# Segment 0 by query tiles, its first FFN matmul in halves, group priorities in the instruction list, and PSUM pairs as tiles of their own

## The chip, the cores and the metric

The kernel runs on 1 core of one Trainium2 chip. The metric is device time of that core in microseconds (us). A time quoted for a kernel is the median of its runs. Engines: PE is TensorE, PEld its weight loads, DVE VectorE, ACT ScalarE, POOL GpSimd, SP SyncE.

## The reference, cut to what matters

```python
# x: 2048 tokens of 576; 32 heads of 18; 4 segments of 512 tokens
h  = x + A(layernorm(x))                 # memory attention, below
h2 = h + gelu(layernorm(h) @ w1 + b1) @ w2 + b2        # 576 -> 4608 -> 576

# A, for each segment s in order:
p     = softmax(q_s @ k_s.T * scale + causal mask)
a_dot = p @ v_s
a_mem = phi(q_s) @ M / (phi(q_s) @ z + 1e-6)           # M = z = 0 in segment 0
o     = g * a_mem + (1 - g) * a_dot                    # g = sigmoid(beta)
M, z  = M + phi(k_s).T @ v_s, z + sum(phi(k_s))
# all o, concatenated, @ wo
```

Segment 0 has no memory term, so its attention can be computed for any query tile of 128 tokens as soon as the keys up to that tile are there.

## The kernel before

The file does not write instructions in their final order. It builds a graph of operations, each with a priority, a cost per engine, what it comes after and which buffers it takes. A list scheduler, which runs on the host while the kernel is built, plays the graph through with these costs and fixes the order on each engine; the instructions are then emitted in that order, and on the chip PE kept to it. The order is decided by the costs written in the file, not by what happens on the chip. This is the list's choice between operations that could start:

```python
def add(self, prio, cost, fn, after=(), acq=None, use=(), table=None, size=0, name=""):
    op = Op(prio, cost, fn, after, acq, ...)
# [cut] in schedule(): for each ready operation, e = engine that would finish it first,
# t0 = when it could start there
b = best.get(e)
if b is None:
    best[e] = (t0, op)
elif t0 <= max(free[e], b[0]) + 1e-9 and t0 >= b[0] - 1e-9:     # equal start: priority decides
    if op.prio < b[1].prio:
        best[e] = (t0, op)
elif t0 < b[0]:                                                 # else the earlier start
    best[e] = (t0, op)
# [cut]
if e == "sp":                                                   # a DMA: one channel of 270 GB/s
    dma = max(dma, op.end) + op.size / 270e3
    op.end = dma + 1.4
```

The first k and q projections are evicted in pairs of PSUM banks, and the two pairs are slices of the tile that later holds the scores:

```python
st_s = Slots([psum.tile([P, 4, 512], F32, name="st")])
pr_s = Slots([st_s.tiles[0][:, 0:2, :], st_s.tiles[0][:, 2:4, :]])
```

Attention of a segment is 20 steps: in each, PE writes scores of 2048 columns to `st`, ACT takes their exponential (1.88 us) to one of three `pt` buffers, DVE or POOL masks the diagonal, and PE multiplies with v. A step holds one or two groups of 4 heads, all four query tiles of them. There are 80 such exponentials, and they serve below as milestones ("the 34th exponential"). The first FFN matmul of a segment needs all four token tiles:

```python
for fg in range(NF // 4):                       # [cut] w1 loaded in 9 groups
    for j in range(4):
        def fn(e, w1=w1, j=j, c=c):
            for k in range(KT):
                nc.tensor.matmul(out=c.t[:], lhsT=w1.t[0:kk, k, j*P:(j+1)*P], rhs=x2T[s].t[0:kk, k, :], ...)
        a = add(pf, {"pe": 1.085}, fn, [la, lb, lc] + x2_ok[s] + ..., c, [w1, x2T[s]], name="F1")
```

The softmax here doesn't subtract the row's maximum and nothing guards it: scores larger than these inputs give would overflow.

Of the kernel before, what the change touches and what calls it, by code (L numbers as in the profile page):

```python
# [33 lines left out]
class Buf:  # L34


    def __init__(self, home):
        self.home, self.left, self.end, self.n = home, 0, 0.0, None
# [14 lines left out]
class Op:  # L53
    def __init__(self, prio, cost, fn, after, acq, use, table, size, name):
        self.prio, self.cost, self.fn, self.acq, self.use = prio, cost, fn, acq, use
        self.table, self.size, self.name = table, size, name
        self.after = [a for a in flat(after) if a is not None]
        self.left, self.then, self.end, self.eng, self.start = 0, [], None, None, None
        self.behind, self.bulk, self.bias = None, False, {}


class Graph:


    def __init__(self):
        self.ops = []

    def add(self, prio, cost, fn, after=(), acq=None, use=(), table=None, size=0, name=""):
        acq = [b for b in (acq if isinstance(acq, list) else [acq]) if b is not None]
        op = Op(prio, cost, fn, after, acq, [b for b in use if b is not None], table, size, name)  # L70
        for b in op.use + acq:
            b.left += 1
        self.ops.append(op)
        return op

    def schedule(self):
# [6 lines left out]
        table, dma = None, 0.0  # L83
# [9 lines left out]
        while ready:  # L93
            best = {}
            for op, at in ready.items():
                lo = max([0.0] + [b.home.soonest() for b in op.acq])
# [3 lines left out]
                for e, t in at.items():  # L100
                    t0 = max(free[e], t, lo, dma - 1.0 if op.bulk else 0.0)
                    c = op.cost[e]
                    done = t0 + c + op.bias.get(e, 0.0)
                    if pick is None or done < pick[2]:
                        pick = (e, t0, done)
                e, t0, _ = pick
                b = best.get(e)
                if b is None:
                    best[e] = (t0, op)
                elif t0 <= max(free[e], b[0]) + 1e-9 and t0 >= b[0] - 1e-9:  # L110
                    if op.prio < b[1].prio:
                        best[e] = (t0, op)
                elif t0 < b[0]:
                    best[e] = (t0, op)
            assert best, "no operation can start"
# [7 lines left out]
            if e == "sp":  # L123
                dma = max(dma, op.end) + op.size / 270e3
                op.end = dma + 1.4
            for b in op.acq:
                b.n = min(range(len(b.home.free)), key=lambda i: b.home.free[i])
                b.home.free[b.n] = INF
# [22 lines left out]
def kernel(  # L151
# [33 lines left out]
    BIG = 3.0e38  # L185
    X_PRIO = 4.0
    MASK_BIAS = 0.6
    BATCHES = (15, 30, 36)
    VEC = dict(dve=nc.vector, pool=nc.gpsimd)

# [13 lines left out]
    x_s = slots(4, [P, D], "x")  # L204
    xT_s = slots(2, [P, KT, L], "xT")
    x2_s = slots(1, [P, KT, L], "x2T")
    oT_s = slots(1, [P, KT, L], "oT")
    qk_s = slots(4, [P, 2, L], "qk")
# [16 lines left out]
    v_augs = [[const.tile([P, H, Dh + 1], BF16, name=f"v_aug{b}_{j}") for j in range(TPS)] for b in range(NSEG)]  # L225
# [10 lines left out]
    hT = const.tile([P, NF, L], BF16, name="hT")  # L236

    early_pool = ExitStack()
    over = early_pool.enter_context(tc.tile_pool(name="over", bufs=1))
    for nm in "kqv":  # L240
        wts[nm] = over.tile([P, KT, D], BF16, name=f"wt_{nm}")
    pad_s = slots(2, [P, G, 2, 4, 32], "qk_pad", pool=over)
    fk_s = slots(5, [P, H, 32], "fk_pad", pool=over)
    xn_s = slots(3, [P, XW], "xn", pool=over)

    def to_w2():
        if not w2_c:
            early_pool.close()
            late = ctx.enter_context(tc.tile_pool(name="late", bufs=1, reuse_waits="tile"))
            w2_c.extend(late.tile([P, WCH, D], BF16, name=f"w2_{c}") for c in range(NF // WCH))  # L250

    warm = pt_s.tiles[0][:, 0, :]
    st_s = Slots([psum.tile([P, 4, 512], F32, name="st")])
    pr_s = Slots([st_s.tiles[0][:, 0:2, :], st_s.tiles[0][:, 2:4, :]])
    ox_s = Slots([psum.tile([P, 512], F32, name="ox")])
    c_s = slots(3, [P, 512], "ps_c", F32, psum)

# [14 lines left out]
    def build(direct):  # L272

        for home in (pad_s, fk_s, xn_s, x_s, xT_s, x2_s, oT_s, qk_s, pt_s, h_s, hc_s, ot_s, e_s, r_s, ek_s, rk_s, t1_s, t2_s,
                     xn2_s, on_s, w1_s, ln_s, r1_s, r2_s, pr_s, st_s, ox_s, c_s):
            home.free = [0.0] * len(home.tiles)
        gr = Graph()
        add = gr.add

        def memset(prio, eng, cost, *aps, val=0.0, after=()):  # L280
            def fn(e):
                for ap in aps:
                    VEC[e].memset(ap, val)
# [23 lines left out]
        wst = Buf(st_s)  # L307
# [21 lines left out]
        def load_x(prio, t, after=()):  # L329
            buf = Buf(x_s)  # L330
# [10 lines left out]
        w_ok["v"] = load_w(-7.3, "v", A_wv)  # L341
# [34 lines left out]
        def stage_X(s, prio):  # L376
# [3 lines left out]
            for tl in range(TPS):  # L380
                xb, ld = xs_pre[tl] if s == 0 else load_x(prio + 0.1 * tl, s * TPS + tl)
# [43 lines left out]
        pairs_done, tq, tq_ops = [], {}, {}  # L425
        z_fk, z_va = [], []

        def stage_P(s, prio):
            fk_bufs[s] = []
            for tl in range(TPS):  # L430
                p0 = prio + 0.1 * tl
# [3 lines left out]
                for n, nm in ((1, "k"), (0, "q")):  # L435
                    if s == 0:
# [8 lines left out]
                    for hf in range(2):  # L445
                        c = Buf(c_s)
                        a = proj(p0, xT, tl, nm, hf, [xn_ok[s, tl]], c)
# [6 lines left out]
                if s == 0:  # L454
                    for g in PE_QK:
                        def fn(e, g=g, tl=tl, pad=pad):
                            ptv = tq[g].t[:].bitcast(BF16).rearrange("p (n q) -> p n q", n=2)
                            for n in range(2):
                                nc.tensor.transpose(out=ptv[:, n, tl * P:(tl + 1) * P], in_=pad.t[:, g, n, :, :].rearrange("p i d -> p (i d)"),
                                                    identity=ident[:])  # L460
                        if tl == 0:
                            tq[g] = Buf(ox_s if g == 0 else c_s)
                        tq_ops.setdefault(g, []).append(add(p0 + 0.05, {"pe": 0.13}, fn, list(evs.values()) + z_pad + tq_ops.get(g, []),
                                                            tq[g] if tl == 0 else None, [pad] + ([] if tl == 0 else [tq[g]]), name="TQ"))
# [3 lines left out]
                st = add(p0 - 0.6, {"sp": 0.5}, lambda e, pad=pad, rows=rows: nc.sync.dma_start(  # L468
# [14 lines left out]
                for hf in range(2):  # L483
                    c = Buf(c_s)
                    a = proj(p0 + (0.6 if s == 0 else 0), xT, tl, "v", hf, [xn_ok[s, tl]], c)
# [5 lines left out]
        def stage_M(s, prio):  # L491
            va = v_augs[s]
# [30 lines left out]
            mz_ok[s] = add(prio, {"dve": 2.8}, blk, accs + later + mz_gates + z_eps, None, [], name="mblk")  # L523
# [3 lines left out]
        oT, oT_ok, exps = {}, {}, []  # L527

        def stage_A(s, prio, prev_done):
            va = v_augs[s]  # L530
# [89 lines left out]
            for g in range(G):  # L620
# [17 lines left out]
                done.append(a)  # L638
            oT[s] = Buf(oT_s)
# [30 lines left out]
        def stage_B(s, prio):  # L670
# [3 lines left out]
            for tl in range(TPS):  # L674
                t = s * TPS + tl
                p0 = prio + 0.1 * tl
                xb, ld = load_x(p0, t, oT_ok[s][:1])
                h = Buf(h_s)
                prev = None
                for hf in range(2):  # L680
                    c = Buf(c_s)
                    a = proj(p0, oT[s], tl, "o", hf, oT_ok[s], c)
# [19 lines left out]
        f2_chunks = {}  # L702
        tok = Slots([None, None])

        def stage_C(s, prio):
            ready_f = {}
            pend = []
            for fg in range(NF // 4):
                w1 = Buf(w1_s)
                fcols = slice(fg * 512, (fg + 1) * 512)  # L710
                la = load(prio - 1 + 0.01 * fg, lambda w1=w1: w1.t[:, 0:4, :], lambda fcols=fcols: B_w1[0:512, fcols].rearrange("(k p) f -> p k f", p=P),
                          524e3, begin, acq=w1)
                lb = load(prio - 1 + 0.01 * fg, lambda w1=w1: w1.t[0:64, 4, :], lambda fcols=fcols: B_w1[512:576, fcols], 66e3, use=[w1])
                lb.behind = la
                lc = load(prio - 1 + 0.01 * fg, lambda w1=w1: w1.t[64:KTAIL, 4, :], lambda fcols=fcols: b1v[:, fcols], 1e3, use=[w1])
                lc.behind = la
                for j in range(4):
                    f = fg * 4 + j
                    c = Buf(c_s)
                    pf = prio + 0.001 * f  # L720

                    def fn(e, w1=w1, j=j, c=c):
                        for k in range(KT):
                            kk = KTAIL if k == 4 else P
                            nc.tensor.matmul(out=c.t[:], lhsT=w1.t[0:kk, k, j * P:(j + 1) * P], rhs=x2T[s].t[0:kk, k, :], start=(k == 0), stop=(k == 4))  # L725
                    a = add(pf, {"pe": 1.085}, fn, [la, lb, lc] + x2_ok[s] + f2_chunks.get((s - 1, f), []), c, [w1, x2T[s]], name="F1")
                    if s >= direct:
                        ready_f[f] = add(pf - 12, {"act": 0.60}, lambda e, f=f, c=c: nc.scalar.activation(  # L728
                            out=hT[:, f, :], in_=c.t[:], func=ACT.Gelu_apprx_tanh), [a, exps[-1]], None, [c], table="gelu", name="gelu1")
                        continue  # L730
                    ev = copy(pf - 16, 0.61, 0.69, lambda f=f: hT[:, f, :], lambda c=c: c.t[:], [a], None, [c])
                    pend.append(ev)
                    if f + 1 in BATCHES:
                        f0 = f + 1 - len(pend)
# [141 lines left out]
```

## Time and profile before

| | before |
|---|---|
| time, median of 3 runs | 493.79 us (493.7 to 494.58) |
| span of the profiled run | 489.6 us |
| PE busy | 467.3 us, 95% |
| PE work, priced start to start (estimate, below) | 451.7 us |
| so PE waits (in that run) | 37.9 us |

The page of the kernel before: busy time, then the span in 40 slices of 12.2 us (tenths busy; PEclk is the granted PE clock in tenths), then the chain of waits that ended last. The profiled run took 491.34 us.

```profile
PE 467.3 (95%) x4581; PEld 298.7 (61%) x4604; DVE 254.2 (52%) x622; ACT 294.7 (60%) x288; POOL 126.4 (26%) x222
...
PE   6789889979999999999999999999999999999997
...
PEclk9999989988999999999999999999999999999999
DMA  8599996365699794953487671234664112440110
...
PE 79%; DVE 9%; ACT 6%; issue 2%; POOL 2%; DMA 2%; SPq 0%; DVEq 0%; ACTq 0%
```

PE is the limit, and it is loose only in the first ten or so slices, where the clock also drops twice. Stretches of the same kernel show who paces that part (busy us of each engine in the stretch, instruction counts in brackets, then clock, DMA share and GB/s):

```profile
core 0: us, PE busy (x) PEld busy (x) DVE busy (x) ACT busy (x) POOL busy (x), PEclk, DMA share, GB/s
29.90:132.00 102.10, 93.27 (x1318) 65.83 (x1317) 84.58 (x224) 88.25 (x97) 49.36 (x80) 0.95 0.78 188
60.00:100.00 40.00, 37.65 (x519) 26.83 (x520) 31.54 (x77) 32.86 (x35) 17.28 (x28) 0.96 0.71 168
140.00:180.00 40.00, 39.60 (x338) 19.92 (x342) 26.87 (x51) 36.32 (x23) 7.09 (x11) 1.00 0.93 248
```

PE's busy time overstates its work, because the records of successive matmuls overlap: one of 288 columns has a mean length of 0.286 us, and the next starts 0.1225 us after it. I therefore price each matmul by the distance between starts in dense parts of the timeline (288 columns 0.1225 us, 512 columns 0.217, a value matmul 0.026, a transpose 0.056, a step of scores 0.33) and add these up in PE's instruction order. The start of an exponential minus the work in front of its scores is how long PE has waited by then. It is an estimate.

The timeline of PE, then of ACT, at the first projections (start, duration, operation; in brackets the idle time before it and what ended it):

```profile
8.59 2.63 PE L420 MATMUL st<-wt_k,xT_68 128*128 128x288 bf16 x20
11.95 1.39 PE L420 MATMUL st<-wt_q,xT_68 128*128 128x288 bf16 x10 [0.73 <-ACT qk_pad_149 L300]
14.25 1.39 PE L420 MATMUL st<-wt_q,xT_68 128*128 128x288 bf16 x10 [0.92 <-DVE qk_pad_150 L302]
```

```profile
11.25 0.64 ACT L300 CAST qk_pad_149<-st 128x576 bf16<-128x576 f32 x1 [1.77 <-PE st L420]
```

The 20 matmuls are the k pairs of two token tiles. The eviction of the first pair starts at 11.25 us, when both have ended, although its own ten ended about 1.2 us sooner; then PE waits for evictions. They alternate where they could overlap.

### The profile page before, as it was taken

What the parts mean: (1) busy time and instruction counts of PE and PEld (TensorE: products, weight loads), DVE (VectorE), ACT (ScalarE), POOL (GpSimd) and SP (SyncE); (2) the same over time, 40 slices, a digit from 0 to 9 for tenths busy, and PEclk for the clock granted to TensorE, in tenths of its full rate; (3) what the DMA queues carried; (4) which work ended last, traced back from release to release, by engine and by line L of the source; (5) the groups of instructions that cost most, each with busy time, mean ns of one, the idle gap of its engine ahead of it and who ended that gap; (6) DMA issues with size and microseconds to landing.
All of it is one profiled execution on the core that took longest, in us unless ns stands there. A gap on an engine that the chain in (4) does not pass through costs nothing.

```text
span 489.6 us, 11245 instructions
## 1 busy us (share of the span) xinstructions
PE 467.3 (95%) x4581; PEld 298.7 (61%) x4604; DVE 254.2 (52%) x622; ACT 294.7 (60%) x288; POOL 126.4 (26%) x222
## 2 busy tenths in 40 slices
PE   6789889979999999999999999999999999999997
PEld 3566657757544466777554457686445776445775
DVE  7788877898666678556679743528000111000111
ACT  2489979868889896766878897603554001555000
POOL 4645634473332115333436101202000000000000
PEclk9999989988999999999999999999999999999999
DMA  8599996365699794953487671234664112440110
GB/s 256 176 228 233 263 161 190 126 171 146 189 278 256 230 242 138 184 119 92 137 210 192 191 194 37 59 80 166 194 173 141 42 37 72 146 138 9 37 36 25
DMA packets 105916, 73.39 MB, mean 150 GB/s; under 512 B 61668, under 2 KB 99720, under 8 KB 105864
## 3 DMA queue, kind: packets, MB, share of 16 engines
q1 hardware_dynamic: 105864, 72.67, 56.2%
q8 instruction: 36, 0.59, 0.5%
q14 instruction: 16, 0.13, 0.1%
HBM read 38.83 MB, written 20.71 MB: 122 GB/s over the span
## 4 chain that ended last, share of the span: by engine, by line
PE 79%; DVE 9%; ACT 6%; issue 2%; POOL 2%; DMA 2%; SPq 0%; DVEq 0%; ACTq 0%
PE ps_c_163 L761 11%; PE ps_c_162 L725 10%; PE ps_c_163 L725 10%; PE ps_c_161 L725 10%; PE ps_c_161 L761 9%; PE ps_c_162 L761 7%; PE ox L612 6%; PE st L578 4%; PE ps_c_162 L409 3%; PE ps_c_161 L409 3%; PE ps_c_163 L409 2%; ACT hT L735 2%; PE st L420 2%; ACT pt_76 L582 1%; DMA qk_74<-qkd_167 1%
## 5 line engine op out<-in xcount | busy, mean ns | idle before, releaser
L761 PEld LDWEIGHTS <-hT 128*128 128x128 bf16 x1152 | 110.5, 98 | 27.9
L582 ACT ACTIVATE pt_77<-st 128x2048 bf16<-128x2048 f32 x27 | 50.8, 1881 | 12.6 <-PE st L578 8.9
L582 ACT ACTIVATE pt_76<-st 128x2048 bf16<-128x2048 f32 x27 | 50.7, 1879 | 9.4 <-PE st L578 7.3
L582 ACT ACTIVATE pt_78<-st 128x2048 bf16<-128x2048 f32 x26 | 48.8, 1878 | 11.3 <-PE st L578 9.8
L728 ACT ACTIVATE hT<-ps_c_162 128x512 bf16<-128x512 f32 x24 | 14.3, 598 | 46.7 <-PE ps_c_162 L725 46.7
L593 POOL TENSOR_SCALAR_AFFINE_SELECT pt_76<-pt_76 128x512 bf16<-128x512 bf16 x34 | 23.8, 711 | 61.8 <-ACT pt_76 L582 61.8
L725 PEld LDWEIGHTS <-w1g_101 128*128 128x128 bf16 (+1 forms) x240 | 22.9, 97 | 27.4 <-issue 0.2
L725 PEld LDWEIGHTS <-w1g_100 128*128 128x128 bf16 (+1 forms) x240 | 22.5, 97 | 26.2 <-issue 0.2
L725 PEld LDWEIGHTS <-w1g_99 128*128 128x128 bf16 (+1 forms) x240 | 22.4, 97 | 25.9 <-issue 0.9
L593 POOL TENSOR_SCALAR_AFFINE_SELECT pt_77<-pt_77 128x512 bf16<-128x512 bf16 x32 | 22.6, 714 | 46.2 <-ACT pt_77 L582 44.6
L593 POOL TENSOR_SCALAR_AFFINE_SELECT pt_78<-pt_78 128x512 bf16<-128x512 bf16 x30 | 21.6, 726 | 44.9 <-ACT pt_78 L582 43.1
L735 ACT ACTIVATE hT<-hT 128x7680 bf16<-128x7680 bf16 (+1 forms) x6 | 31.7, 5318 | 0.0
L409 PEld LDWEIGHTS <-xT_69 128*128 128x128 bf16 (+1 forms) x240 | 21.8, 99 | 8.8 <-issue 3.2
L773 DVE TENSOR_TENSOR ot_84<-ps_c_162,hc_82 128x288 bf16<-128x288 f32 x3 | 1.4, 455 | 46.4 <-PE ps_c_162 L761 46.4
L773 DVE TENSOR_TENSOR ot_84<-ps_c_163,hc_82 128x288 bf16<-128x288 f32 x6 | 2.7, 454 | 41.7 <-PE ps_c_163 L761 41.7
L728 ACT ACTIVATE hT<-ps_c_161 128x512 bf16<-128x512 f32 x24 | 14.3, 598 | 12.0 <-PE ps_c_161 L725 12.0
L728 ACT ACTIVATE hT<-ps_c_163 128x512 bf16<-128x512 f32 x24 | 14.3, 597 | 11.5 <-PE ps_c_163 L725 11.5
L612 PEld LDWEIGHTS <-pt_76 128*128 128x128 bf16 x432 | 15.6, 96 | 8.7 <-issue 3.5
L612 PEld LDWEIGHTS <-pt_77 128*128 128x128 bf16 x432 | 15.6, 96 | 7.1 <-issue 3.7
L612 PEld LDWEIGHTS <-pt_78 128*128 128x128 bf16 x416 | 15.0, 96 | 7.6 <-issue 5.1
L409 PEld LDWEIGHTS <-xT_68 128*128 128x128 bf16 (+1 forms) x160 | 15.4, 100 | 4.5 <-DMA xT_68<-xnd_172 0.2
L409 PEld LDWEIGHTS <-oT_71 128*128 128x128 bf16 (+1 forms) x160 | 15.1, 97 | 4.0 <-issue 0.2
(491 smaller groups left out, 1030.2 us busy)
## 6 DMA issues: line engine op xcount, KB each, us to landing
w1g_99<-in_B_w_dram SPq DMA_DIRECT2D x12, 512.0 KB
w1g_100<-in_B_w_dram SPq DMA_DIRECT2D x12, 512.0 KB
w1g_101<-in_B_w_dram SPq DMA_DIRECT2D x12, 512.0 KB
hc_82<-hd SPq DMA_DIRECT2D x8, 288.0 KB
hc_83<-hd SPq DMA_DIRECT2D x8, 288.0 KB
hd<-h_79 SPq DMA_DIRECT2D x6, 288.0 KB
hd<-h_80 SPq DMA_DIRECT2D x5, 288.0 KB
hd<-h_81 SPq DMA_DIRECT2D x5, 288.0 KB
```

Of the source, the lines that this page charges most:

```text
L409: nc.tensor.matmul(out=c.t[:, 0:HALF], lhsT=xTb.t[0:kk, k, ts], rhs=wt[0:kk, k, cs], start=(k == 0), stop=(k == 4))
L420: nc.tensor.matmul(out=c.t[:, hf, 0:HALF], lhsT=xTb.t[0:kk, k, ts], rhs=wt[0:kk, k, hf * HALF:(hf + 1) * HALF], start=(k == 0), stop=(k == 4))
L578: nc.tensor.matmul(out=st.t[:, i, off:off + n_], lhsT=qk[rows, 1, kt * P:(kt + 1) * P], rhs=qk[rows, 0, kt * P:L], start=True, stop=True, ...
L582: ex = add(ps, {"act": 1.88}, lambda e, st=st, pt=pt: nc.scalar.activation(out=pt.t[:], in_=st.t[:], func=ACT.Exp, scale=scale), [sc], pt, ...
L593: nc.gpsimd.affine_select(out=blk, in_=blk, pattern=[[0, 4], [1, P]], compare_op=ALU.is_ge, fill=0.0, base=0, channel_multiplier=-1)
L612: nc.tensor.matmul(out=oxv[:, qt, i, :], lhsT=pt.t[:, i, o:o + P], rhs=va[kt][:, 4 * g + i, :], start=fresh and qt == qts[0] and i == 0, s ...
L725: nc.tensor.matmul(out=c.t[:], lhsT=w1.t[0:kk, k, j * P:(j + 1) * P], rhs=x2T[s].t[0:kk, k, :], start=(k == 0), stop=(k == 4))
L728: ready_f[f] = add(pf - 12, {"act": 0.60}, lambda e, f=f, c=c: nc.scalar.activation(out=hT[:, f, :], in_=c.t[:], func=ACT.Gelu_apprx_tanh) ...
L735: ge = add(2.9, {"act": 0.44 * len(pend)}, lambda e, f0=f0, f=f: nc.scalar.activation(out=hT[:, f0:f + 1, :], in_=hT[:, f0:f + 1, :], func ...
L761: nc.tensor.matmul(out=c.t[:, 0:HALF], lhsT=hT[:, f, tl * P:(tl + 1) * P], rhs=w2_c[ch][:, f - ch * WCH, hf * HALF:(hf + 1) * HALF], start ...
L773: o = add(p2 - 16, {"dve": 0.46}, lambda e, cs=cs, c=c, ot=ot, hc=hc: nc.vector.tensor_tensor(out=ot.t[:, cs], in0=c.t[:, 0:HALF], in1=hc. ...
```

## The change

Its intent is to give PE something to do early: start attention sooner, and let FFN work of segment 0 run among the first attention steps. It has four parts.

1. **List.** Every group of operations gets an offset on its priority (74 numbers in a table), and among operations that start within a "patience" of the earliest one the priority decides. Loads are modelled with about seven in flight.
2. **Query tiles.** Segment 0's attention goes query tile by query tile, in halves of 16 heads: 20 steps of 16 score matmuls of 128 columns. Tiles 0 and 1 are transposed on PE, tiles 2 and 3 by 8 transposing loads of 131 KB, off the path to the first exponential.
3. **Halves.** Segment 0's first FFN matmul runs in two halves of 256 tokens, w1 being read twice. The gelu of each half goes in two batches.
4. **Own tiles.** The early pairs get two PSUM tiles of their own; the tile of scores is opened in the same space afterwards. Some clearings move or go to ACT, and three chunks of w2 are loaded early.

The diff, cut to its core:

```diff
     def add(self, prio, cost, fn, ...):
+        prio += self.offsets.get(self.tag + name, 0.0)
...
-                b = best.get(e)
-                if b is None: ...                      # (cut, shown above)
+                cand.setdefault(e, []).append((t0, op))
+            best = {}
+            for e, ops in cand.items():
+                soon = min(t0 for t0, _ in ops) + self.patience.get(e, 0.0) + 1e-9
+                best[e] = min((a for a in ops if a[0] <= soon), key=lambda a: (a[1].prio, a[0]))
...
             if e == "sp":
+                flying = sorted(flying)[-7:]
+                t0 = max(t0, flying[0] if len(flying) > 6 else 0.0)
...
+    HALVES = (18, 36)
+    OFFSETS = {"A00copy": 15.76, "A00st0": -30.59, "A01st0": 161.83, ...}      # (cut)
+    PATIENCE = {'act': 0.069, 'dve': 0.073, 'pool': 0.521}
...
-    st_s = Slots([psum.tile([P, 4, 512], F32, name="st")])
-    pr_s = Slots([st_s.tiles[0][:, 0:2, :], st_s.tiles[0][:, 2:4, :]])
+    pr_s = slots(2, [P, 2, 512], "pr", F32, pr_pool)
+    st_s = Slots([None])                                # opened by to_st() at the first scores
...
+        def stage_A0(prio):                             # segment 0
+            for qt in range(TPS):
+                for Q in range(2):
+                    for kt in [qt] + list(range(qt)):
+                        def score(e, ...):
+                            for b in range(4):
+                                for i in range(4):
+                                    nc.tensor.matmul(out=st.t[:, i, b * P:(b + 1) * P], lhsT=kk[rows, 4 * Q + b, 1, ks],
+                                                     rhs=qq[rows, 4 * Q + b, 0, qs], ...)
...
         def stage_C(s, prio):
+            for half in ((0, 1) if s == 0 else (None,)):
+                x2_in = x2_ok[s] if half is None else x2_ok[s][2 * half:2 * half + 2]
+                # (cut) w1 loaded again for half 1; matmuls of 256 columns; gelu in batches of HALVES
```

## The prediction

> **What bounds it.** The page gives PE 467.3 of 489.6 us busy, and the chain that ended last is 79% PE. I priced PE's work by start-to-start times from the timeline: 288-column matmul 0.1225 us, 512-column 0.217, value matmul 0.026, transpose 0.056, one score step 0.33. With the instruction order that gives about 452 us of work. So PE waits about 38 us, and only that can be won. Comparing this sum with the start of each of the 80 attention exponentials (1.88 us each) places it: about 8.5 us before the first one (29.9 us), 19 from there to the 34th (132.0 us), 7 up to 318 us, about 3 at the end (last output). In the stretch 29.9 to 132.0 ACT is busy 88.3 of 102.1 us (view of stretches), DVE 84.6: ACT and DVE pace it, 3.09 us per exponential, and PE has only about 83 us to do. PE is so thin there that the clock was granted at half for 3.4 us (from 65.8) and 6.8 us (from 106.8). The Trainium skill, "TensorE: Matmul & The Clock Gate", Part 1: an idle window of about 3.4 us halves the clock; both lengths agree. Cost about 5 us.
>
> **What the change does.**
> 1. Early pairs as own tiles. In the timeline ACT's first eviction of k begins at 11.25 us, when the second pair ended (11.23), though its own pair ended about 1.2 us earlier: PE and evictors alternate (waits of 0.7, 0.9, 0.9 us on PE). Own tiles let them overlap: about 3 us. Three 0.31 us clearings leave the space between the first two normalisations: 1 us more. Query tiles 2 and 3 leave the path to the first exponential: about 5 us of projections move behind it. First exponential at about 21 us instead of 29.9; PE's wait before it about 4 instead of 8.5 us.
> 2. Query tiles, halved first FFN matmul. PE work hardly changes: 720 matmuls become 900, but 360 have 256 columns (estimate 0.109 us each, half of 0.217; the weight load, mean 97 ns, still hides). Score steps of segment 0 become 16 matmuls of 128 columns: estimate +2 us in all. PE total about 454. But 180 half matmuls and the output projections can start after two query tiles and stand, in instruction order, among exponentials 12 to 34: PE work between exponentials 1 and 34 rises from 83 to about 105 us.
> 3. ACT gets work there as well: evictions, and two gelu batches with table changes (about 6.5 us each, from the 6.18 us batch of 7680 and 1.28 us per load). Summed by order, ACT has about 111 us there against 93. At the old ratio (93 in 102) the stretch takes about 120 us; PE then waits 12 to 17 us, not 19.
> 4. Cost: w1 is read twice for segment 0, 5.3 MB more; stores and transposing loads of segment 0 halve. DMA share after 132 us is 0.68: hidden.
> 5. Priorities by group: no cost; at most a few us.
>
> **Sum.** Waits of 4 + 15 + 6 + 3 = 28 instead of 38, plus 2 us of work: about 8; a few more if a half-clock period disappears.
>
> **Predicted: 483.5 us (475 to 491); faster by over 2% 0.50, within 2% 0.47, slower 0.03.**
>
> **Right if** the first exponential starts at 20 to 23 us, PE's first k, q pairs overlap their evictions, the half clock shows for under 7 us, the 34th exponential starts at 136 to 145 us, the stretch after 330 us looks as before.
>
> **Wrong if** the transposing loads for tiles 2 and 3 land late and stall the seventh exponential; the gelu batches stall PE; weights kept in the FFN buffer create false waits; or ACT and DVE run nearly without gaps (then about 476).

## The result

The changed kernel takes 480.05 us (4 runs, 479.82 to 480.33), beside 493.75 us of the kernel before in the same job (4 runs, 491.93 to 494.58). The ratio is 0.9728, with a 95% interval of 0.97 to 0.9755: faster by over 2%. A ratio here is the mean time of one kernel's fast runs over that of the other's of the same rounds, so it is not quite the ratio of the medians quoted.

The page of the changed kernel:

```profile
PE 463.3 (97%) x4974; PEld 317.2 (66%) x4992; DVE 256.4 (54%) x611; ACT 301.8 (63%) x302; POOL 123.0 (26%) x200
...
PE   7989889999999999999999999999999999999997
...
PEclk9999999999999999999999999999999999999999
DMA  8859899999969996566577655324645352450110
...
PE 82%; DVE 6%; DMA 3%; ACT 3%; POOL 2%; issue 2%; SPq 1%; ACTq 0%; DVEq 0%; POOLq 0%
```

PE's slices are fuller early, and the clock no longer drops before the end. In the chain DVE and ACT have smaller shares (9 and 6%, now 6 and 3%), DMA has 3 instead of 2%. The same stretches of the changed kernel:

```profile
core 0: us, PE busy (x) PEld busy (x) DVE busy (x) ACT busy (x) POOL busy (x), PEclk, DMA share, GB/s
29.90:132.00 102.10, 96.85 (x1504) 75.76 (x1500) 88.41 (x219) 90.26 (x94) 41.22 (x60) 1.00 0.97 234
60.00:100.00 40.00, 38.05 (x626) 31.07 (x625) 32.62 (x75) 35.01 (x32) 13.65 (x21) 1.00 0.99 229
140.00:180.00 40.00, 40.00 (x514) 31.68 (x513) 21.94 (x47) 32.83 (x26) 13.32 (x18) 1.00 1.00 248
```

Look at the last column but one. From 29.9 to 132 us the DMA engines were busy for 0.78 of the time before and are for 0.97 after; from 140 to 180 us, where w1 is read in both kernels, 0.93 and 1.00. How much room is left this share does not say: it is summed from records and is no ceiling. The 1.00 stands beside 248 GB/s, and the same stretch of e8 below has 1.06 and 290 GB/s.

The timeline of PE, then of ACT, in the changed kernel:

```profile
8.31 1.41 PE L464 MATMUL pr_151<-hT,xT_70 128*128 128x288 bf16 x10
9.55 1.40 PE L464 MATMUL pr_150<-hT,xT_70 128*128 128x288 bf16 x10
10.79 1.39 PE L464 MATMUL pr_151<-hT,xT_70 128*128 128x288 bf16 x10
```

```profile
9.75 0.64 ACT L344 CAST qk_pad_134<-pr_151 128x576 bf16<-128x576 f32 x1 [0.66 <-PE pr_151 L464]
...
21.21 1.90 ACT L612 ACTIVATE pt_75<-st 128x2048 bf16<-128x2048 f32 x1
```

The first eviction now begins when its own ten matmuls end, PE's pairs follow each other without a wait, and the first exponential starts at 21.2 us instead of 29.9. PE's waits, by the accounting above:

| PE waits, us | before | predicted | after |
|---|---|---|---|
| before the first exponential | 8.5 | 4 | 4.3 |
| to about 139 us | 19.3 | 15 | 12.8 |
| to the 80th exponential | 6.7 | 6 | 4.8 |
| after it | 3.4 | 3 | 3.4 |
| sum | 37.9 | 28 | 25.2 |
| PE work | 451.7 | +2 | +1.2 (452.9) |
| clock at half (start and end aside) | 10.2 | under 7 | 0 |

So the time came from where it was predicted to come from. That does not yet show *which part of the change* brought it.

### The profile page after: what moved, and what is told of

The parts are those of the page before. It is cut to its first block, busy times and chain, and to the rows that moved or that the text cites. A ratio compares the mean times of both kernels' runs of the same rounds, so it can differ in the third digit from the quotient of the medians.

```text
span 478.1 us, 12029 instructions
## 1 busy us (share of the span) xinstructions
PE 463.3 (97%) x4974; PEld 317.2 (66%) x4992; DVE 256.4 (54%) x611; ACT 301.8 (63%) x302; POOL 123.0 (26%) x200
## 4 chain that ended last, share of the span: by engine, by line
PE 82%; DVE 6%; DMA 3%; ACT 3%; POOL 2%; issue 2%; SPq 1%; ACTq 0%; DVEq 0%; POOLq 0%
PE ps_c_146 L878 12%; PE ps_c_146 L928 12%; PE ps_c_145 L878 11%; PE ps_c_145 L928 9%; PE ps_c_144 L878 8%; PE ps_c_144 L928 8%; PE ox L750 5%; PE st L716 4%; PE ps_c_144 L453 3%; PE ps_c_145 L453 3%; PE ps_c_146 L453 3%; DMA w1g_98<-in_B_w_dram 1%; DMA w_lo<-qkd_154 1%; SPq L338 1%; DMA qkd_155<-qk_pad_135 1%
## 5 line engine op out<-in xcount | busy, mean ns | idle before, releaser
L720 ACT ACTIVATE pt_75<-st 128x2048 bf16<-128x2048 f32 x20 | 37.6, 1878 | 11.6 <-PE st L716 8.1
L720 ACT ACTIVATE pt_76<-st 128x2048 bf16<-128x2048 f32 x20 | 37.6, 1878 | 9.4 <-PE st L716 6.4
L720 ACT ACTIVATE pt_77<-st 128x2048 bf16<-128x2048 f32 x20 | 37.6, 1880 | 8.4 <-PE st L716 5.1
L878 PEld LDWEIGHTS <-w1g_99 128*128 128x128 bf16 x300 | 28.1, 97 | 21.8 <-issue 0.4
L878 PEld LDWEIGHTS <-w1g_100 128*128 128x128 bf16 x300 | 28.2, 97 | 21.5 <-issue 0.2
L878 PEld LDWEIGHTS <-w1g_98 128*128 128x128 bf16 x300 | 27.9, 97 | 20.7 <-issue 0.4
L897 ACT ACTIVATE hT<-hT 128x4608 bf16<-128x4608 bf16 (+2 forms) x7 | 32.0, 4589 | 0.1
L928 PE MATMUL ps_c_146<-w_lo,hT 128*128 128x288 bf16 x234 | 32.0, 286 | 0.0
L940 DVE TENSOR_TENSOR ot_83<-ps_c_144,hc_81 128x288 bf16<-128x288 f32 x5 | 2.3, 454 | 50.6 <-PE ps_c_144 L928 50.6
L731 POOL TENSOR_SCALAR_AFFINE_SELECT pt_76<-pt_76 128x512 bf16<-128x512 bf16 x24 | 18.6, 782 | 38.0 <-ACT pt_76 L720 38.0
L453 PEld LDWEIGHTS <-xT_71 128*128 128x128 bf16 (+1 forms) x240 | 21.7, 97 | 7.9 <-issue 2.6
L731 POOL TENSOR_SCALAR_AFFINE_SELECT pt_75<-pt_75 128x512 bf16<-128x512 bf16 x24 | 17.3, 729 | 33.9 <-ACT pt_75 L720 33.8
L731 POOL TENSOR_SCALAR_AFFINE_SELECT pt_77<-pt_77 128x512 bf16<-128x512 bf16 x24 | 17.4, 734 | 28.6 <-ACT pt_77 L720 28.6
L928 PE MATMUL ps_c_145<-w_lo,hT 128*128 128x288 bf16 x180 | 24.7, 286 | 0.0
L716 PE MATMUL st<-qk 32*128 32x512 bf16 (+3 forms) x384 | 23.8, 301 | 0.0
L346 DVE CAST hT<-ps_c_145 128x512 bf16<-128x512 f32 x19 | 13.1, 692 | 18.0 <-PE ps_c_145 L878 18.0
L928 PE MATMUL ps_c_144<-w_lo,hT 128*128 128x288 bf16 x162 | 22.8, 286 | 0.0
L453 PEld LDWEIGHTS <-xT_70 128*128 128x128 bf16 (+1 forms) x200 | 18.6, 97 | 5.6 <-issue 0.9
```

The lines of the kernel that those rows point to most:

```text
L346: VEC[e].tensor_copy(out=dst(), in_=src())
L453: nc.tensor.matmul(out=c.t[:, 0:HALF], lhsT=xTb.t[0:kk, k, ts], rhs=wt[0:kk, k, cs], start=(k == 0), stop=(k == 4))
L716: nc.tensor.matmul(out=st.t[:, i, off:off + n_], lhsT=qk[rows, 1, kt * P:(kt + 1) * P], rhs=qk[rows, 0, kt * P:L], start=True, stop=True, ...
L720: ex = add(ps, {"act": 1.88}, lambda e, st=st, pt=pt: nc.scalar.activation(out=pt.t[:], in_=st.t[:], func=ACT.Exp, scale=scale), [sc], pt, ...
L731: nc.gpsimd.affine_select(out=blk, in_=blk, pattern=[[0, 4], [1, P]], compare_op=ALU.is_ge, fill=0.0, base=0, channel_multiplier=-1)
L878: nc.tensor.matmul(out=c.t[:, u * n_:(u + 1) * n_], lhsT=w1.t[0:kk, k, j * P:(j + 1) * P], rhs=x2T[s].t[0:kk, k, ts], start=(k == 0), stop ...
```

## The experiments

My theory was the prediction's: query tiles and the halved matmul feed PE, and own tiles start it sooner. The rival: much of the gain is the order that the tuned list makes, and the structure matters little. All twelve runs gave correct results. "Waits" are listed in the order of the table above.

| run | us | ratio to before (95%) | waits | half clock, us |
|---|---|---|---|---|
| after | 480.05 | 0.9728 (0.97 to 0.9755) | 4.3 / 12.8 / 4.8 / 3.4 | 0 |
| e1 after, pairs in one tile | 480.36 | 0.9767 (0.9713 to 0.9821) | 6.7 / 10.5 / 4.8 / 3.4 | 0 |
| e2 before, own tiles | 487.76 | 0.9912 (0.9867 to 0.9957) | 4.6 / 19.7 / 6.2 / 3.4 | 10.2 |
| e3 after, no early half | 489.13 | 0.9938 (0.9888 to 0.9988) | 4.2 / 24.8 / 1.8 / 3.4 | 6.8 |
| e4 after, no offsets | 495.17 | 1.006 (1.0009 to 1.011) | 5.8 / 20.5 / 11.2 / 4.1 | 17.1 |
| e5 before, own tiles, tuned list | 477.10 | 0.9675 (0.9633 to 0.9717) | 4.7 / 11.1 / 3.9 / 3.6 | 0 |
| e6 as e3, re-tuned | 483.59 | 0.9792 (0.9757 to 0.9827) | 4.2 / 20.9 / 0.3 / 3.5 | 3.4 |
| e7 after, one gelu batch per half | 480.47 | 0.9738 (0.9704 to 0.9773) | 4.2 / 12.8 / 5.3 / 3.5 | 3.4 |
| e8 after, more DMA | 485.92 | 0.9848 (0.9805 to 0.9891) | 4.2 / 14.6 / 8.6 / 3.3 | 6.8 |
| e9 as e5, no offsets | 504.62 | 1.0203 (1.0144 to 1.0263) | 4.5 / 34.8 / 8.9 / 3.4 | 30.7 |
| e10 as e5, five offsets | 481.44 | 0.9753 (0.9713 to 0.9793) | 4.8 / 15.4 / 4.4 / 3.6 | 3.4 |
| e11 after, offsets of my own | 483.41 | 0.9796 (0.9754 to 0.9839) | 5.8 / 14.6 / 5.5 / 3.4 | 3.4 |
| e12 as e5, another search | 480.87 | 0.9742 (0.97 to 0.9784) | 8.2 / 10.9 / 3.7 / 3.5 | 3.4 |

e1 to e4 shared one job, e5 to e8 a second, e9 to e12 a third; the changed kernel had its own. Differences between jobs are differences of medians; the kernel before has 493.75, 493.37, 493.09 and 492.60 us in the four, so they carry an error of about one microsecond.

### e1: the changed kernel with its pairs in one tile again

```diff
-    pr_s = slots(2, [P, 2, 512], "pr", F32, pr_pool)
+    pr_one = pr_pool.tile([P, 4, 512], F32, name="pr")
+    pr_s = Slots([pr_one[:, 0:2, :], pr_one[:, 2:4, :]])
```

> The changed kernel with the two early PSUM pairs again as slices of one tile; same instruction order. Theory (a pair's eviction waits for the other pair's matmuls only because they share a tile): ACT's first eviction of k starts about 11.0 us instead of 9.75, the first exponential about 24 us instead of 21.2, the time 2 to 4 us longer (482 to 484). Rival (the early stretch is set by loads and by ACT's own copies): first exponential within 0.7 us of 21.2, time within 1 us.

Measured 480.36 us, against 480.05 of the changed kernel. The alternation is back; PE, then ACT, in the timeline of e1:

```profile
8.30 2.64 PE L465 MATMUL pr<-hT,xT 128*128 128x288 bf16 x20
11.67 1.39 PE L465 MATMUL pr<-hT,xT 128*128 128x288 bf16 x10 [0.73 <-ACT qk_pad L345]
```

```profile
10.98 0.64 ACT L345 CAST qk_pad<-pr 128x576 bf16<-128x576 f32 x1 [1.90 <-PE pr L465]
```

The first exponential starts 2.4 us later (23.6 us), yet the 11th is only 1.0 us late (59.1 against 58.1) and the 21st is level (95.1 against 95.0). The mechanism of point 1 is real and worth nothing here: what PE no longer waits at the start it waits later. One such later wait stands in the changed kernel's chain of waits, followed back from 46.5 us (start, duration, what; SPq is SP issuing loads, L338 the transposing ones):

```profile
36.78 1.89 SPq L338
...
38.71 1.49 SPq L338
40.24 5.07 DMA w_lo<-qkd_154
45.31 0.05 issue
45.35 0.23 PE st L608 x4
```

The scores of the 7th exponential wait until 45.31 us for a transposing load of tiles 2 and 3. PE fills most of that time with projections, and its wait there is 1.3 us in the changed kernel and 0.5 in e1. The rest of the 2.4 us is regained in pieces up to the 21st exponential; which wait returns which piece I did not separate.

### e2: the kernel before with own tiles, and nothing else

```diff
-    st_s = Slots([psum.tile([P, 4, 512], F32, name="st")])
-    pr_s = Slots([st_s.tiles[0][:, 0:2, :], st_s.tiles[0][:, 2:4, :]])
+    pr_s = slots(2, [P, 2, 512], "pr", F32, pr_pool)
+    st_s = Slots([None])        # and to_st() at the first scores, as in the change
```

> The kernel before with own tiles for the early pairs and nothing else changed (four more instructions on ACT may move). Theory: first exponential about 27 us instead of 29.9 and the time 2 to 3.5 us shorter (about 490 to 491.5). Rival (ACT and DVE pace what follows, an early lead is lost in their queues): first exponential earlier, time within 1 us of before.

Measured 487.76 us: 5.6 us less than the 493.37 of the kernel before in the same job, and even more than I had expected. (By the ratio of means it is 4.3 us, 2.1 to 6.5; the two profiles differ by 4.0.) The first exponential starts at 26.1 us, and the waits before it fall from 8.5 to 4.6 us; the later ones stay (19.7 against 19.3). In the kernel before nothing takes the gain back, in the changed one something does. The same edit is worth 4 to 6 us in one structure and 0.3, which is nothing within the noise, in the other.

### e3: the changed kernel without the early half

```diff
-                x2_in = x2_ok[s] if half is None else x2_ok[s][2 * half:2 * half + 2]
+                x2_in = x2_ok[s]
```

> The changed kernel, but the first half of the first FFN matmul waits for all four query tiles, so the list puts its first matmul at the 26th instead of the 14th exponential, and projections of later segments in its place. Theory 1 (starting the FFN after two query tiles is what feeds PE): PE waits 5 us or more longer between the first exponential and 140 us, time 485 to 488. Theory 2 (any work does; the list has projections to fill with): time within 2 us of 480.

Measured 489.13 us, 9.1 more than the changed kernel. The waits between the first exponential and 139 us grow from 12.8 to 24.8 us. A hole opens behind the 14th exponential: only 0.54 us of PE work stands in front of the 14th, and the 15th starts 5.12 us after it. So in this structure, with this list, half matmuls among the early steps do feed PE, as predicted. But the offsets were made for a graph that has them; e6 takes that objection up.

### e4: the changed kernel without offsets and patience

```diff
-        gr = Graph(OFFSETS, PATIENCE)
+        gr = Graph({}, {})
```

> The changed kernel with the table of group offsets and the patience empty. Theory 2 (the list priorities are a large part of the gain): 486 us or more. Theory 1 and the prediction's point 5 (priorities are worth a few us at most): 481 to 484.

Measured 495.17 us: slower than the kernel before, and 15.1 us more than the changed kernel. All query tiles, halves and own tiles are still there. The first exponential even starts at 17.3 us, the earliest of all kernels here except e11, which equals it. The clock is at half for 17.1 us; its first such period lies in this stretch:

```profile
17.00:46.00 29.00, 25.94 (x386) 18.91 (x384) 26.20 (x84) 22.45 (x27) 14.32 (x18) 0.82 0.54 148
```

A mean clock of 0.82 at a PE that is busy for 25.94 of 29 us: the slow clock inflates the busy time (in e2, below, five matmuls take 1.41 us at the half clock and 0.78 at the full one). My theory fell here: the changed kernel needs the offsets and patience for its gain, and the prediction had dismissed them. That the structure is worth nothing does not follow. The list's new choice is itself slow without offsets (e9), and the changed structure under the old choice was not run. The next question was whether the list needs the structure.

### e5: the structure of before, own tiles, a tuned list

The kernel before with the new list (part 1), own tiles (part 4's), and 178 offsets of my own. They come from a random search of 14 minutes on the host that minimises the list's own end time, with the costs that stand in the file; nothing was fitted to the chip. Segment 0 keeps its old steps, and w1 is read once.

```diff
+        prio += self.offsets.get(self.tag + name, 0.0)          # and the list's new choice, as in the change
+    OFFSETS = {"A0comb": -181.142, "A0copy": -538.845, ...}       # 178 of them, cut
+    PATIENCE = {'dve': 0, 'act': 0.0505, 'pool': 0, 'pe': 0}
-    pr_s = Slots([st_s.tiles[0][:, 0:2, :], st_s.tiles[0][:, 2:4, :]])
+    pr_s = slots(2, [P, 2, 512], "pr", F32, pr_pool)            # own tiles, as in e2
```

> The kernel before with own pair tiles, the changed kernel's list (group offsets, patience, eight loads in flight) and offsets that I searched for this structure with the list's own costs, 14 minutes of search. Segment 0 by group pairs, its first FFN matmul whole, w1 read once. Theory 1 (query tiles and halves are what feeds PE): tuned or not it stays at 485 or more, PE's wait between the first exponential and 140 us above 15 us. Theory 2 (the priorities carry the gain, and most structures can be tuned to it): 477 to 483, that wait near 12 us and no half clock.

Measured 477.10 us (476.64 to 478.35), ratio 0.9675: faster than both kernels. All of its runs lie under all runs of the changed kernel (from 479.82), but the two ran in different jobs and the intervals of their ratios overlap, so I claim "at least as fast". It needs no query tiles, no halves and no second reading of w1.

e2 and e5 have the same structure and differ in list alone, so they show what the list does. (It also picks the engine of each eviction: ACT has 288 instructions in e2 and 291 in e5, DVE 622 and 615. PE's operations are the same.) By the accounting they have waited equally long up to the 13th exponential (11.5 and 11.6 us). Then come these stretches, of e2 first:

```profile
60.00:70.00 10.00, 7.77 (x85) 4.50 (x82) 6.24 (x18) 7.09 (x6) 3.95 (x7) 0.83 0.84 124
70.00:96.00 26.00, 26.00 (x346) 18.98 (x346) 21.20 (x53) 21.94 (x25) 11.57 (x21) 1.00 0.59 163
96.00:112.00 16.00, 13.12 (x208) 9.60 (x207) 14.93 (x37) 12.52 (x12) 9.27 (x14) 0.79 0.53 132
```

The same stretches of e5:

```profile
60.00:70.00 10.00, 9.49 (x125) 7.04 (x122) 7.86 (x23) 8.58 (x11) 4.33 (x7) 1.00 0.90 207
70.00:96.00 26.00, 26.00 (x373) 19.45 (x370) 23.50 (x55) 22.47 (x26) 11.90 (x19) 1.00 0.63 150
96.00:112.00 16.00, 15.91 (x223) 11.73 (x222) 14.77 (x36) 14.45 (x17) 10.96 (x18) 1.00 0.73 211
```

Between the two holes of e2 both are full. In the holes e2's clock is 0.83 and 0.79, e5's is 1.00. In PE's order, the 14th exponential of e2 has 0.85 us of work in front of it (20 value matmuls), that of e5 2.49 us; the 26th has 1.42 us in e2 and 2.70 in e5. The list of e5 has put projections of later segments there, which e2 did at other times, when PE was full anyway. The total work is the same 451.7 us. The timeline of PE at the first hole in e2:

```profile
61.82 0.26 PE L621 MATMUL ox<-v_aug,pt 128*128 128x19 bf16 x4 [1.12 <-ACT pt L591]
...
62.75 0.41 PE L417 MATMUL ps_c<-wt_k,xT 128*128 128x288 bf16 x2
63.43 0.30 PE L417 MATMUL ps_c<-wt_k,xT 128*128 128x288 bf16 x1 [0.28 <-DMA xT<-xnd]
...
65.56 1.41 PE L417 MATMUL ps_c<-wt_q,xT 128*128 128x288 bf16 x5
```

In e2 PE waits 1.12 us for an exponential with nothing else in its order, then for the input of the next projections to land, and five matmuls take 1.41 us at the half clock where they take 0.78 at the full one. In e5 four groups of k and q projections run from 60.2 to 64.0 us, each at 0.77 or 0.78 us.

### e6: no early half, list re-tuned

The edit of e3 with offsets searched anew on the host.

```diff
-                x2_in = x2_ok[s] if half is None else x2_ok[s][2 * half:2 * half + 2]
+                x2_in = x2_ok[s]
-    OFFSETS = {...}                    # the change's
+    OFFSETS = {...}                    # of a search for this graph
```

> The late half of e3 with offsets searched for it (14 minutes, from the changed kernel's). Theory 1: it stays at 487 to 489. Theory 2 (e3 lost because its offsets fitted another order): 480 to 484.

Measured 483.59 us. Of the 9.1 us that e3 lost, 5.5 came back by order alone. So once the list is made for it, what remains for the early half in this structure is 3.5 us and not 9; and as e11 and e12 will show, one search can miss another by as much, so even the 3.5 are not shown to be the half's. Undoing one part under a list tuned for the whole overstates the part.

### e7: one gelu batch for each half

```diff
-    HALVES = (18, 36)
+    HALVES = (36,)                     # and offsets searched for it
```

> The changed kernel with one gelu batch of 36 tiles per half of segment 0 instead of two of 18, offsets searched again. It takes away two pairs of table loads (1.28 us each[...]) from ACT in the stretch that ACT and DVE pace. Theory 2: 476 to 480. Rival (the longer batch holds back the exponentials by 12 us at a time and PE runs dry): 481 or more.

The Trainium skill, "ScalarE: Activation LUTs", section "What ACT_TABLE_LOAD costs", gives about 1.28 us for a load and with a drain about 2.66 us for every switch to another table set. The traces agree with the load: each is 1.283 us, 14 of them in the changed kernel and 10 in e7 (and 10 before). They do not agree with the 2.66 us. In the changed kernel an exponential ends at 85.15 us, and then ACT runs:

```profile
85.16 1.28 ACT L897 ACT_TABLE_LOAD   x1
86.46 4.04 ACT L897 ACTIVATE hT<-hT 128x4608 bf16<-128x4608 bf16 x1
```

From the end of one activation to the start of the next a switch takes 1.31 us, and 145 of the 160 loads that lie between two activations in these traces stay under 1.45. Four switches fewer are thus 5.2 us of ACT. Measured: 480.47 us, the same as the changed kernel; neither the expected gain nor the rival's loss came. But e7 also has the offsets of another search, and such a search can be 3 to 4 us off (e11, e12): that ACT's switches are off the path is not shown by it.

### e8: the changed kernel with more DMA

```diff
+                    if half == 1:      # each w1 group of half 1 is also copied to a spare DRAM buffer
+                        nc.sync.dma_start(out=w1.t[:, 0:4, :], in_=B_w1[0:512, fcols]...)
+                        nc.sync.dma_start(out=w1x[fg][:, :], in_=B_w1[0:512, fcols])
```

> The changed kernel, with 4.7 MB of w1 read once more to DRAM during the loads of the second half, instruction order of PE, ACT and DVE the same. If the second read of w1 is hidden, as predicted: within 1 us of 480. If the DMA engines set the pace there: 483 or more.

Measured 485.92 us, 5.9 more. A stretch of e8, to be set beside the third row of the changed kernel:

```profile
140.00:180.00 40.00, 36.75 (x479) 28.55 (x477) 19.71 (x44) 29.68 (x25) 10.46 (x16) 1.00 1.06 290
```

The 9 copies of 524 KB (4.7 MB) go out with the second reading, three from 97 to 103 us and six from 144 to 170. From 140 to 180 us PE was busy throughout in the changed kernel (40.00) and is for 36.75 us here, with the DMA share at 1.06. The longest wait of PE for a load there, as the trace lists it (total, times, longest), is for a group of w1:

```profile
PE ps_c L884 <- DMA w1g<-in_B_b_dram: 1.9, 1, 1.9
```

In the changed kernel no wait of PE (the list has those over 0.15 us) from 60 to 318 us ends with a load. The waits up to 139 us grow by 1.8 us and those from there to the 80th exponential by 3.8. The Trainium skill, "DMA: Bandwidth & Descriptors", section "Issuing engines are not separate DMA queues", says that DMAs run on the same 16 engines and interleave with each other, whichever engine starts them; no run here tests that, since SP issues every transfer of these kernels. By this run another transfer of nearly the size of the second reading of w1 (5.3 MB) is not hidden. Whether the bytes or SP's time for issuing (7.2 us for the nine copies, in the queue of all other loads) costs the 5.9 us is not separated. How much the second reading itself costs this does not measure: the copies also write to DRAM, and they come on top of it.

### e9, e10: how much of e5 is its offsets

e9 is e5 with the new list but no offsets; e10 keeps five of the 178, chosen on the host by the list's own end time.

```diff
-    OFFSETS = {"A0comb": -181.142, ...}            # e5
+    OFFSETS = {}                                   # e9
+    OFFSETS = {"A2comb": 19.569, "P00Pq": 31.101, "P01TQ": 35.969,
+               "P1Pq": 0.044, "P3copy": -74.969}   # e10
```

> The structure of e5 (the kernel before, own pair tiles) with the new list, its patience on ACT and no offsets. If the new list's rules alone made e5 fast: 477 to 484. If the offsets did: as slow as e4 or slower, 491 to 500, with a long wait of PE between the first exponential and 140 us and half-clock periods again.

> The same with five offsets kept of the 178 of e5: the last transposes of early keys and queries later, segment 1's query projections a little later, two more. If the gain is the closing of two holes in PE's work (near the 13th and the 25th exponential) and no sum of many small things: 479 to 484 and under 4 us of half clock. If many offsets are needed: 486 or more.

Measured 504.62 and 481.44 us. The same operations under three lists take 504.62, 481.44 and 477.10 us (ACT has 285, 291 and 291 instructions, so the engine of a few evictions changes too): the offsets are worth 27.5 us (the first and the last ran in different jobs), and five of them bring 23.2. The new choice in the list is thus no gain by itself. In this structure it is even slower than the old choice (e2, 487.76). From e2, the new choice and the offsets together gain 10.7 us (other jobs); offsets under the old choice were not run.

### e11, e12: equal search for both structures

Is the structure of before faster, or did e5's search have luck? Both graphs were searched from zero, by the same program, for 25 minutes each.

```diff
-    OFFSETS = {...}                    # the change's (e11), e5's (e12)
+    OFFSETS = {...}                    # of the new search
```

> The changed kernel with offsets that I searched from none (25 minutes), to set against its own. If structures can be tuned to about the same time: 478 to 484, near its own 480. If its own offsets were a lucky find: 486 or more.

> The structure of e5 with offsets of another search from none (25 minutes). If e5's 477 is what this structure gives when tuned: 476 to 481. If e5 was a lucky find: 483 or more. With e11 this sets two tuned lists of each structure side by side.

Measured 483.41 us for the changed structure and 480.87 for that of before. A search's luck is 3.4 us (e11 against the changed kernel) and 3.8 us (e12 against e5). With equal search the structure of before is 2.5 us faster. These two kernels do differ: they shared a job, and no run of one (482.56 to 484.54) reaches the other (479.79 to 481.66). But the difference is smaller than the luck of a search, so it says nothing sure of the structures. So query tiles and halves bring no gain that these runs can show once the list is tuned:

| us | list without offsets | tuned lists |
|---|---|---|
| structure of before, own tiles | 504.62 (e9) | 477.10 (e5), 480.87 (e12) |
| changed structure | 495.17 (e4) | 480.05 (after), 483.41 (e11) |

Untuned, the changed structure was 9 us faster (in different jobs, and e9 keeps ACT's patience, which e4 does not); tuned, it is some 3 us slower, which is within the luck of a search. The gains of structure and order do not add. They seem to fill the same holes: the 14th and 26th exponentials have 2.7 and 2.5 us of work in front of them in the changed kernel, 2.5 and 2.7 in e5.

## Why the prediction was right or wrong

The time was predicted at 483.5 us (475 to 491) and is 480.05. The terms of the sum: waits of 28 us predicted, 25.2 measured; additional work 2, measured 1.2. The largest miss is in the stretch up to 139 us, 15 predicted and 12.8 measured, and the next in the stretch behind it, 6 and 4.8. The number came near because the prediction summed PE's work in the order that the changed file gives, so the offsets' effect was in the sum without being named. The 105 us of work that it counted between the first and 34th exponential are 105.0 in the trace at the same prices (82.6 before). The sum could not say which part earns this: in e5 only 89.4 us stand between the same two exponentials, and PE waits no longer (11.1 against 12.8 us up to 139 us).

**Right, and shown.** PE is the limit, and only its waits could be won. The first exponential starts at 21.2 us (20 to 23 predicted), the 34th at 139.1 (136 to 145); the k and q pairs overlap their evictions; the half clock is gone (under 7 us predicted); the waits after the 80th exponential are 3.4 us in both kernels. The score steps of 16 matmuls, for which I had put part of the 2 us, cost 0.335 us, and the old ones 0.33. One event of its "wrong if" list did occur, but small: the seventh exponential waited for a transposing load, and PE for 0.9 us with it (e1).

**Wrong: point 5, "Priorities by group: no cost; at most a few us."** This is the step that failed. Without offsets and patience the changed kernel takes 495.17 us and gains nothing over the kernel before (e4); on the old structure offsets are worth 27.5 us under the new list (e9, e5), and list and offsets together 10.7 us over the old list (e2, e5). Why I missed it: I took the order as given and asked what each part costs and what it feeds. But an order that puts 0.85 us of PE work in front of one exponential and 3.8 in front of another wastes what the total could cover. The numbers were in the trace before: the 14th and 26th exponential have 0.85 and 1.42 us of work in front of them, and the clock falls to half just there (from 65.8 and from 106.8 us). I had read "PE is so thin there" as a lack of work. Work from elsewhere in the order was enough to fill it.

**Wrong in its cause: point 2, query tiles and half matmuls as what fills PE.** They do fill it in this structure (e3, e6), by about 9 us under the given list and at most some 3.5 under one made for the graph. But later segments' projections fill the same holes as well (e5, e12). The predicted mechanism works with the offsets, not without them (e4), and it is not necessary.

**Half wrong: point 1, "Own tiles let them overlap: about 3 us."** In the changed kernel the end of the overlap is worth 0.3 us, within noise (e1); in the kernel before it is worth 4 to 6 (e2). I added up gains at the start as if each reached the end. The start of the first exponential ranks nothing: it lies at 17.3 us in e4 (495.17 us) and e11 (483.41), at 21.2 in the changed kernel (480.05), at 26.7 in e5 (477.10) and at 29.6 in e12 (480.87).

**Left undecided: point 4, "DMA share after 132 us is 0.68: hidden."** The share is 0.68 after the change too (132 to 318 us), and no wait of PE from 60 to 318 us ends with a load, which speaks for it. But the reason given was weak. That share was a mean over 186 us (to 318 us). Where w1 is read it was 0.93 already in the kernel before (140 to 180 us), and it is 1.00 there after; 4.7 MB more beside the second reading cost 5.9 us (e8). And with the halves six of the nine groups of the first reading moved to between 69 and 91 us, and three of the second to between 98 and 107; from 60 to 100 us the share rose from 0.71 to 0.99. What the second reading costs by delaying other loads stays unmeasured.

**How much is the clock?** I had said about 5 us. In the 21 runs of the kernel before that stand beside the experiments, a straight line of time against half-clock time (from each run's mean clock) has a slope of 0.31 us per us and meets zero half clock at 488.7 us; the correlation is 0.85. That makes about 4 of the 13.7 us. It is a correlation: a run with longer waits also gets a slower clock, and no run took the clock alone away.

**Left open.** Which of the five offsets of e10 matters, whether a longer search would part the two structures, and what the changed structure takes under the old list, I did not test.

## What to carry to other kernels

When a kernel's order is made by a list with written costs, tune the order before the structure, and test a structural change with a list made for it: here five priority numbers under the new list, with own tiles, took the old structure to 481.44 us, beside 480.05 for the whole change, and undoing a part under the other's list overstated it (9.1 against at most 3.5 us). Count the work in front of each milestone in the bounding engine's order: a thin place beside full ones may be work in the wrong place, and a remedy by reordering costs no bytes. A gain at the start counts only if no later gate (here, in part, a transposing load) takes it back; check it at the 10th and 20th milestone, not at the first.

## What the Trainium skill lacked or had wrong

- "TensorE: Matmul & The Clock Gate", Part 1, puts the half clock down to at least one idle window of about 3.4 us, and its table of rules asks for no gaps over about 3 us. The lengths agree (3.4 and 6.8 us in the kernel before), the condition does not: in all 21 drops over these runs (those at the very end aside), PE was busy by its records for 0.39 to 2.24 us of the 3.41 us window ahead of the drop, and its longest gap there was 0.6 to 2.4 us. What these windows share is little array time (an estimate: columns at the page's 2.4 GHz, matmuls of 32 rows counted as a quarter): 0.12 to 1.35 us. Windows at the full clock without a drop had 1.26 us or more, those of the first 10 us aside; the two ranges overlap a little, so this gives no exact threshold. A thin window is enough; it need not be idle. The page tells of the like in another kernel, where frequent micro-idles between groups of matmuls make the clock oscillate ("A second HAM failure mode: psum-queue depth-cycling"), but its table of rules does not take it up.
- "ScalarE: Activation LUTs", "What ACT_TABLE_LOAD costs": its 2.66 us for every switch to another table set are not seen here; a switch took 1.31 us between two activations (e7).
- No page has the value of instruction order on an engine that is 95% busy: the same operations took 504.62, 481.44 and 477.10 us under three lists (e9, e10, e5).
